# Spreading the last row sums by one product, and sharing the last finishes with ScalarE and GpSimd

## The chip, the cores and the metric

The kernel runs on one core of a Trainium2 chip. Its time is the device time of one execution in microseconds (us), and the number that counts is the median of several executions. A profiled execution of the same program gives the trace: what each engine did and when. The engines are TensorE (PE in the profile, its weight loads PEld), VectorE (DVE), ScalarE (ACT), GpSimd (POOL) and SyncE (SP), which here issues nearly all DMA transfers.

## The reference, cut to what matters

The input x has 2048 rows of 512 numbers. Attention with 32 heads of 16 dimensions each is mixed with a routed feed-forward part by a gate per row:

```python
q, k, v = qkv[0], qkv[1], qkv[2]              # 32 heads, Dh = 16
p = softmax(einsum("bhqd,bhkd->bhqk", q, k) * Dh ** -0.5)
a = einsum("bhqk,bhkd->bhqd", p, v).transpose(0, 2, 1, 3).reshape(B, S, D) @ wo
g = sigmoid((x * gate_w).sum(-1, keepdims=True))
return g * a + (1 - g) * b                    # b: x plus a SwiGLU on the two rows with the largest x @ w_r
```

## The kernel before, in words

**Units and steps.** The 32 heads form 16 pairs. A unit is one pair with one half (1024) of the queries, so there are 32 units, u = 0 to 31 (`UNITS` = 32). A unit has 16 steps, one for each block of 128 keys, 512 steps (`STEPS`) in all. A step makes four score products of 128 keys by 512 queries (`s_piece`, line 596: head j, query chunk c), whose exponentials ScalarE writes to a tile `P` (line 597). Two steps later four products with V (`av_mm`, line 605) add to one PSUM tile `av`. Each of the four takes 32 of its 128 rows; in each such group rows 0 to 15 are the output of one head for one chunk of 512 queries, and row 16 is the row sum of the softmax, because V carries a column of ones. Beside that, up to unit 31, "m" pieces (line 528) and VectorE reductions (line 532) find the row maxima of units to come. A written-out order (`ORDER`) interleaves all of these; `at_step(s, f)` hangs other work behind step s, and a generator `fills` gives one piece of output work per slot. Every engine works through its instructions in the order in which the program gives them.

**The drain.** After the last reduction some 20 steps are left. Each consists of 4 score products, 4 products with V and one `wo_last` (line 453: three products that apply the output weights to 128 rows of the result, into the PSUM tile `fl`, which has one buffer), followed by `finish` on VectorE (line 501: acc = ps * gate + acc). In these steps unit 30, the last but one, is normalized: `l_cols` (line 656) brings its row sums onto the partitions by four small products with `sel_l`, takes the reciprocal of 16 columns (line 658), and copies it out to 512 columns (`rx`, line 660). One step later `l_rows` (line 665) turns `rx` back by four products with the identity, and VectorE multiplies (line 667). `last_rows` (line 672) sends the result by DMA into `last_n[0]`, which `split_last` (line 496) reads later.

**The tail.** `tail()` handles unit 31, for which nothing is left to run beside it. `av_out` copies `av` to an SBUF tile `o` on ScalarE (line 618). Then come the small products (line 693), the reciprocal of 16 columns (line 695), six products of `wo_last`'s kind for row tiles 6 and 7 (`pw`), the copy to 512 columns, half on ScalarE and half on VectorE (lines 701, 702), the turning back into two PSUM tiles (line 705), two multiplications (line 708), and the split of `o` into a rounded part and a rest (`onh` on ScalarE, line 67; `onl` on VectorE, line 68). Then ten row tiles of the output are finished by VectorE (line 501) and stored by SP (`store`, line 504, 128 rows of 2 KB each): first tiles 6 and 7, then the eight tiles 8 to 15, each from three products (line 721) of all 128 rows of `onh` or `onl` with `wz`, the rows of `wo` for the last two heads, with zeros for the rows of the other query chunk.

PSUM tiles: `st` has three buffers, `fl`, `av`, `mxb` one each, `mxa` one of two banks. SBUF tiles of the tag "o" share six buffers.

Of the kernel before, what the change touches and what calls it, by code (L numbers as in the profile page):

```python
# [7 lines left out]
F32 = mybir.dt.float32  # L8
F32R = mybir.dt.float32r
U32 = mybir.dt.uint32  # L10
AF = mybir.ActivationFunctionType
# [5 lines left out]
S, D, H, DH, F = 2048, 512, 32, 16, 1792  # L17
NG = 4
PAIRS = H // 2
UNITS = PAIRS * 2  # L20
KT = S // 128
VW = DH + 1
# [11 lines left out]
def gated_mix(ctx: ExitStack, tc: tile.TileContext, xT, x, wqkv, wo, w_rg, w_gate, w_up, w_down,  # L34
              consts, pos, out):
    nc = tc.nc
    ctx.enter_context(tc.manual_schedule())
    cp = ctx.enter_context(tc.tile_pool(name="cp", bufs=1))
    xp = ctx.enter_context(tc.tile_pool(name="xp", bufs=1))
    ring = ctx.enter_context(tc.tile_pool(name="ring", bufs=1))  # L40
# [6 lines left out]
    def st_tile(shape=(128, 512)):  # L47
        return psum.tile(list(shape), F32, tag="st", name="st", bufs=3)

    def fl_tile(shape=(128, 512)):  # L50
        return psum.tile(list(shape), F32, tag="fl", name="fl", bufs=1)

    def mxa_tile():
        return psum.tile([128, 2, 512], F32, tag="mxa", name="mxa", bufs=1)

    def mxb_tile(shape=(128, 512)):
        return psum.tile(list(shape), F32, tag="mxb", name="mxb", bufs=1)

    def av_tile():
        return psum.tile([128, 512], F32, tag="av", name="av", bufs=1)  # L60

    def o_tile(name, shape, dt=F32):
        return ring.tile(shape, dt, tag="o", name=name, bufs=6)

    def split(hi, lo, src, scale=None, lo_engine=None):
        if scale is None:
            nc.scalar.activation(hi, src, AF.Copy)
            (lo_engine or nc.vector).tensor_sub(lo, src, hi.bitcast(F32))
        else:
            nc.scalar.activation(hi, src, AF.Copy, scale=scale)  # L70
            nc.vector.scalar_tensor_tensor(lo, src, scale, hi.bitcast(F32), op0=OP.mult, op1=OP.subtract)
# [3 lines left out]
        nc.gpsimd.tensor_sub(lo, src, hi.bitcast(F32))  # L75


    cst = cp.tile([128, 135], F32, name="cst")
    ident, sel_j, sel_l, row0 = cst[:, :128], cst[:, 128:130], cst[:, 130:134], cst[:, 134:135]
    V = cp.tile([128, KT, H * VW + 15], F32, name="V")  # L80
    Kx = [cp.tile([128, S], F32R, name=f"Kx{i}") for i in range(2)]
    Qx = [cp.tile([128, S // 2], F32R, name=f"Qx{i}") for i in range(3)]
# [1 line left out]
    gg = cp.tile([128, 16], F32, name="gg")  # L84
# [320 lines left out]
    acc = []  # L405
# [45 lines left out]
    def wo_terms(ps, ah, al, c, sl, first, last):  # L451
        for n, (a, b) in enumerate(((ah, wop[0]), (al, wop[0]), (ah, wop[1]))):
            nc.tensor.matmul(ps, a[:, sl], b[:a.shape[0], c, :], start=first and n == 0, stop=last and n == 2)  # L453
# [30 lines left out]
    lastp = {}  # L484
# [14 lines left out]
    def finish(t, ps):  # L499
        a = acc[t // 4][:, t % 4, :]  # L500
        nc.vector.scalar_tensor_tensor(a, ps, gg[:, t:t + 1], a, op0=OP.mult, op1=OP.add)  # L501

    def store(t):
        nc.sync.dma_start(out[t * 128:t * 128 + 128, :], acc[t // 4][:, t % 4, :])
# [11 lines left out]
    MX, P, AV = {}, {}, {}  # L516
# [82 lines left out]
    def av_mm(s):  # L599
        u, kt = divmod(s, KT)  # L600
        if kt == 0:
            AV[0] = av_tile()
        for ct in range(4):
            h = (u // 2) * 2 + ct // 2
            nc.tensor.matmul(AV[0][32 * ct:32 * ct + 32, :], V[:, kt, h * VW:h * VW + 32], P[s][:, ct, :],  # L605
                             start=kt == 0, stop=kt == KT - 1)
        del P[s]

# [41 lines left out]
        a = last_n[half][:96, q * 512:q * 512 + 512]  # L650
        nc.gpsimd.tensor_mul(a, a, AV["rb", half, q])

    def l_cols(u):
        ps = mxa_tile()[:, 0, :16]
        for c in range(4):
            nc.tensor.matmul(ps[:, 4 * c:4 * c + 4], AV[u][:, c * 128:c * 128 + 128], sel_l, start=True, stop=True)
        r = ring.tile([128, 16], F32, tag="r16", name="r16", bufs=2)
        nc.vector.reciprocal(r, ps)
        AV["rx"] = o_tile("rx", [128, 16, 32])
        nc.vector.tensor_copy(AV["rx"], r[:, :, None].to_broadcast([128, 16, 32]))  # L660

    def l_rows(u):
        ps = mxa_tile()[:, 0]
        for c in range(4):
            nc.tensor.matmul(ps[:, c * 128:c * 128 + 128],
                             AV["rx"][:, 4 * c:4 * c + 4].rearrange("p a b -> p (a b)"), ident, start=True, stop=True)
        nc.vector.tensor_mul(AV[u], AV[u], ps)

    def last_rows():
        for ct in range(4):  # L670
# [3 lines left out]
    wz = []  # L674

    def load_wz(part):
        if part == 0:
            wz.append(ring.tile([128, 2, 2, 512], F32R, tag="xs", name="wz", bufs=2))
            nc.gpsimd.memset(wz[0].bitcast(F32), 0.0)
            return  # L680
        for i in range(2):
            for ct in range(4):
                j, c = divmod(ct, 2)
                nc.sync.dma_start(wz[0][32 * ct:32 * ct + 16, i, c].bitcast(F32),
                                  wop[i][96 + 16 * j:112 + 16 * j, 3].bitcast(F32))

    def tail():
        u = UNITS - 1
        hl = [o_tile(n, [128, 512], F32R) for n in ("onh", "onl")]
        o = AV[u]  # L690
        ps = st_tile((128, 16))
        for c in range(4):
            nc.tensor.matmul(ps[:, 4 * c:4 * c + 4], o[:, c * 128:c * 128 + 128], sel_l, start=True, stop=True)
        r = ring.tile([128, 16], F32, tag="r16", name="rl", bufs=2)
        nc.vector.reciprocal(r, ps)
        rx = o_tile("rxl", [128, 16, 32])
        pw = [st_tile() for _ in range(2)]
        for t in range(2):
            wo_terms(pw[t], lastp[0][0], lastp[0][1], 3, slice((6 + t) * 128, (7 + t) * 128), True, True)
        rb = r[:, :, None].to_broadcast([128, 16, 32])  # L700
        nc.scalar.activation(rx[:, 0:8], rb[:, 0:8], AF.Copy)
        nc.vector.tensor_copy(rx[:, 8:16], rb[:, 8:16])
        pr = [mxb_tile((128, 256)), fl_tile((128, 256))]
        for c in range(4):
            nc.tensor.matmul(pr[c // 2][:, c % 2 * 128:c % 2 * 128 + 128],
                             rx[:, 4 * c:4 * c + 4].rearrange("p a b -> p (a b)"), ident, start=True, stop=True)
        for t in range(2):
            nc.vector.tensor_mul(o[:, 256 * t:256 * t + 256], o[:, 256 * t:256 * t + 256], pr[t])
        for t in range(2):
            sl = slice(256 * t, 256 * t + 256)  # L710
            split(hl[0][:, sl], hl[1][:, sl], o[:, sl])
        for t in range(2):
            finish(6 + t, pw[t])
            store(6 + t)
        two = mxa_tile()
        for c in range(4):
            sl = slice(c * 128, c * 128 + 128)
            for k in range(2):
                ps = (st_tile, lambda: two[:, 0], st_tile, mxb_tile, st_tile, lambda: two[:, 1], st_tile, fl_tile)[2 * c + k]()
                for n, (a, b) in enumerate(((0, 0), (1, 0), (0, 1))):  # L720
                    nc.tensor.matmul(ps, hl[a][:, sl], wz[0][:, b, k, :], start=n == 0, stop=n == 2)
                finish(8 + 4 * k + c, ps)
                store(8 + 4 * k + c)


    fill, now = {}, [0]
# [1 line left out]
    def at_step(s, f, *a):  # L728
        fill.setdefault(s, []).append((f, a))
# [88 lines left out]
    for t in range(6):  # L818
        at_step(STEPS - 6 + t, wo_last, t, 128)
    at_step(400, load_wz, 0)  # L820
    at_step(404, load_wz, 1)

    def p_v(s):
        if not 0 <= s < STEPS:
            return
        av_mm(s)
        if s % KT < KT - 1:
            return
        u, s = s // KT, now[0]
        av_out(u)  # L830
        if u % 8 == 7 and u < 24:
            for i in range(8):
                at_step(s + 6 + i, l_out, u // 8, i)
        elif u == UNITS - 3:
            for i in range(8):
                at_step(s + 3 + i // 2, l_out, 3, i)
            for half in (1, 0):
                for q in range(2):
                    at_step(s + 10 - half, l_last, half, q)
                    at_step(s + 12 - half, n_last, half, q)  # L840
        elif u == UNITS - 2:
            at_step(s + 1, l_cols, u)
            at_step(s + 2, l_rows, u)
            at_step(s + 3, last_rows)

    def start_step(s):
# [30 lines left out]
    while count["m"] < UNITS * EL:  # L877
        for o in ORDER:
            if o == "s":
                s, i = divmod(count["s"], 4)  # L880
# [15 lines left out]
    for s in range(count["s"] // 4, STEPS + 2):  # L896
        if s < STEPS:
            start_step(s)
            for i in range(4):
                s_piece(s, 1 - i % 2, i // 2)  # L900
        p_v(s - 2)
        next(fills, None)
        end_step(s)
    end_step(STEPS + 2)
    assert next(parts, 0) == 0 and not fill and next(fills, 0) == 0, fill
    tail()


# [29 lines left out]
```

## Time and profile before

| | us |
|---|---|
| time, median of 3 runs (lowest to highest) | 1450.44 (1449.56 to 1451.87) |
| the profiled execution's own time | 1449.58 |
| its span, first to last instruction | 1447.8 |
| PE busy | 1430.4 |
| VectorE busy | 1299.6 |
| ScalarE busy | 1164.5 |
| GpSimd busy | 302.6 |

The 1.78 us between the profiled execution's time and its span lie around the first and the last instruction. A timeline row gives the start, the length, engine, line, operation and what it writes and reads; in brackets stands how long the engine had been idle and what ended that. A row of the groups gives a count, the busy time in all, the mean length of one in ns, and the idle time before them. The chain of waits is followed back from the last instruction to what released each step.

### The profile page before, as it was taken

To read this page: it belongs to the slowest core of one execution; us is meant where nothing else is said; L and a number is where in the kernel's file an instruction comes from. 1 tells how busy PE (TensorE), PEld (TensorE's weight loads), DVE (VectorE), ACT (ScalarE), POOL (GpSimd) and SP (SyncE) were. 2 spreads that over 40 slices of the span, in tenths; PEclk is the share of its full clock that TensorE was granted. 3 is DMA by queue.
4 is the path that set the end of the run, shared out by engine and by line. 5 is a ranking of instruction groups with operands and counts; after the bars stand their busy time and mean duration, and the time that the engine had idled before them with its cause. 6 is when DMAs were issued, how large, how long until landed. Compare 5 with 4: busy or idle time off the path is not lost.

```text
span 1447.8 us, 24210 instructions
## 1 busy us (share of the span) xinstructions
PE 1430.4 (99%) x9141; PEld 636.1 (44%) x9141; DVE 1299.6 (90%) x1541; ACT 1164.5 (80%) x2262; POOL 302.6 (21%) x321
## 2 busy tenths in 40 slices
PE   8999999999999999999999999999999999999998
PEld 5654444444444444444444433334444444444434
DVE  5779999999999999999999999999999999999933
ACT  4467888888888888888888888888888888888874
POOL 3652101020010002000010000326322231232120
PEclk9999999999999999999999999999999999999999
DMA  8702121212014121221314242231212120111003
GB/s 264 196 19 63 34 52 45 53 45 51 28 60 114 61 53 31 52 68 50 83 41 107 84 110 67 45 113 51 52 45 53 40 54 20 37 33 38 18 16 117
DMA packets 53476, 92.72 MB, mean 64 GB/s; under 512 B 12972, under 2 KB 24300, under 8 KB 51856
## 3 DMA queue, kind: packets, MB, share of 16 engines
q1 hardware_dynamic: 53264, 91.17, 23.9%
q8 instruction: 72, 1.18, 0.4%
q14 instruction: 44, 0.36, 0.1%
q0 software_dynamic: 96, 0.01, 0.0%
HBM read 63.64 MB, written 28.56 MB: 64 GB/s over the span
## 4 chain that ended last, share of the span: by engine, by line
PE 94%; DMA 2%; DVE 1%; SPq 1%; ACT 1%; issue 0%; POOL 0%; DVEq 0%; ACTq 0%; POOLq 0%
PE av L605 34%; PE st L596 23%; PE mxa L528 12%; PE mxb L528 10%; PE fl L149 6%; PE fl L453 4%; PE st L248 3%; ACT P L597 1%; DMA xs<-xT 1%; SPq L587 1%; PE mxa L555 1%; DVE Mr L532 1%; DMA wvs<-wqkv 0%; PE fl L352 0%; DVE acc L501 0%
## 5 line engine op out<-in xcount | busy, mean ns | idle before, releaser
L597 ACT ACTIVATE P<-st 128x512 f32<-128x512 f32 x2028 | 1065.0, 602 | 217.4 <-PE st L596 127.7
L532 DVE TENSOR_REDUCE Mr<-mxa 128x2 f32<-128x1024 f32 x655 | 794.7, 1213 | 3.9 <-PE mxa L528 3.4
L605 PE MATMUL av<-P,V 128*32 128x512 f32 x4096 | 545.5, 605 | 0.0
L596 PE MATMUL st<-Qx,Kx 50*128 50x512 f32 x2028 | 539.7, 444 | 4.1 <-ACT P L597 3.6
L532 DVE TENSOR_REDUCE Mr<-mxb 128x1 f32<-128x512 f32 x654 | 451.8, 691 | 69.5 <-PE mxb L528 20.1
L596 PEld LDWEIGHTS st<-Qx,Kx 50*128 50x128 f32 x2028 | 280.8, 184 | 238.8 <-ACT P L597 215.2
L528 PE MATMUL mxb<-Kx,Qx 48*128 48x512 f32 x654 | 325.2, 497 | 0.0
L528 PE MATMUL mxa<-Kx,Qx 48*128 48x512 f32 x1310 | 299.2, 420 | 1.0 <-DVE Mr L532 0.8
L528 PEld LDWEIGHTS mxb<-Kx,Qx 48*128 48x128 f32 x654 | 119.5, 183 | 273.7 <-DVE Mr L532 255.2
L528 PEld LDWEIGHTS mxa<-Kx,Qx 48*128 48x128 f32 x1310 | 126.6, 183 | 46.3 <-DVE Mr L532 7.8
L605 PEld LDWEIGHTS av<-P,V 128*32 128x32 f32 x4096 | 80.9, 108 | 146.0 <-issue 140.0
L164 POOL TENSOR_SCALAR ev<-pe 128x512 fp32r<-128x512 f32 x24 | 35.8, 1490 | 375.3 <-ACT pe L163 375.3
L74 POOL TENSOR_SCALAR hl<-m 128x16 fp32r<-128x16 f32 x32 | 8.1, 253 | 384.1 <-DVE m L571 384.0
L420 POOL TENSOR_TENSOR acc<-acc,w 128x512 f32<-128x512 f32 x32 | 41.0, 1281 | 197.4 <-ACT w L419 197.4
L149 PE MATMUL fl<-xh,wh 128*128 128x512 f32 x96 | 42.9, 447 | 0.0
L149 PE MATMUL fl<-xh,wl 128*128 128x512 f32 x96 | 39.6, 413 | 0.0
L453 PE MATMUL fl<-woh,ahl 128*128 128x512 f32 x96 | 35.2, 447 | 0.0
L501 DVE SCALAR_TENSOR_TENSOR acc<-fl,gg,acc 128x512 f32<-128x512 f32 x15 | 11.3, 750 | 26.4 <-PE fl L453 26.4
L560 DVE TENSOR_REDUCE Mr<-mxa 128x2 f32<-128x1024 f32 x21 | 25.7, 1223 | 9.8 <-PE mxa L555 9.8
L149 PE MATMUL fl<-xl,wh 128*128 128x512 f32 x96 | 31.3, 420 | 0.0
L165 POOL TENSOR_TENSOR ev<-pe,ev 128x512 fp32r<-128x512 f32 x24 | 30.8, 1283 | 2.0
L250 ACT ACTIVATE V<-st 128x512 f32<-128x512 f32 x16 | 9.6, 598 | 25.0 <-PE st L248 24.9
(177 smaller groups left out, 780.5 us busy)
## 6 DMA issues: line engine op xcount, KB each, us to landing
Qx<-q_scr SPq DMA_DIRECT2D x62, 128.0 KB
Kx<-k_scr SPq DMA_DIRECT2D x30, 256.0 KB
k_scr<-ev SPq DMA_DIRECT2D x14, 512.0 KB
q_scr<-ev SPq DMA_DIRECT2D x14, 512.0 KB
xs<-xT SPq DMA_DIRECT2D x16, 256.0 KB
xn<-x SPq DMA_DIRECT2D x4, 1024.0 KB
Qx<-hr SPq DMA_DIRECT2D x256, 2.0 KB
acc<-x_scr SPq DMA_DIRECT2D x4, 1024.0 KB
```

The source lines that it names most:

```text
L149: nc.tensor.matmul(ps, a[:, i, c, :], b[nb][:, c, :], start=n == 0, stop=n == 11)
L164: nc.gpsimd.tensor_scalar(ev[:, 0], t, 1.0, None, op0=OP.mult)
L165: nc.gpsimd.tensor_sub(ev[:, 1], t, ev[:, 0].bitcast(F32))
L248: nc.tensor.matmul(ps, a[nb][:, c, sl], b[:, c, :], start=c == 0 and n == 0, stop=c == 3 and n == 2)
L420: nc.gpsimd.tensor_add(a, a, w)
L453: nc.tensor.matmul(ps, a[:, sl], b[:a.shape[0], c, :], start=first and n == 0, stop=last and n == 2)
L528: nc.tensor.matmul(dst, Qx[u % 3][64 * j:64 * j + 48, t * 128:t * 128 + 128], Kx[(u // 2) % 2][64 * j:64 * j + 48, c * 512:c * 512 + 512], ...
L532: nc.vector.tensor_reduce(Mr[:, g0:g0 + (2 if r == 1 else 1)], MX[r - 1], axis=AX.X, op=OP.max, negate=True)
L560: nc.vector.tensor_reduce(*r, axis=AX.X, op=OP.max, negate=True)
L596: nc.tensor.matmul(ps, k, q, start=True, stop=True)
L597: nc.scalar.activation(P[s][:, 2 * j + c, :], ps, AF.Exp)
L605: nc.tensor.matmul(AV[0][32 * ct:32 * ct + 32, :], V[:, kt, h * VW:h * VW + 32], P[s][:, ct, :], start=kt == 0, stop=kt == KT - 1)
```

## The change

- The constant input `consts` grows from 135 to 259 columns. `sel_l` is now 128 columns wide instead of 4: one product with it puts each group's row sum on all 32 rows of the group.
- Unit 30: `l_cols` goes. `l_rows` is one product with `sel_l`, a reciprocal of 128x512 on VectorE and a multiplication on GpSimd instead of VectorE.
- Unit 31: the same with the product, the reciprocal and the multiplication each in two halves of 256 columns; the multiplication stays on VectorE. The products of row tile 6 move ahead of the wait for `o`, into `fl`; those of row tile 7 stand behind the row-sum product.
- The groups of `av` in unit 31 are put in the order chunk, head, so that each chunk has its rows in one half of the partitions. The 24 output products read 48 rows each, from row 0 or from row 64, and alternate between the two halves. `wz` loses the zero half.
- `finish_two` (ScalarE scales PSUM into an SBUF tile, GpSimd adds it to `acc`) takes the place of `finish` for row tiles 6, 7, 12, 13 and 14; tiles 8 to 11 and 15 stay on VectorE. Stores keep their order: 6, 7, 8, 12, 9, 13, 10, 14, 11, 15.

```diff
-    cst = cp.tile([128, 135], F32, name="cst")
-    ident, sel_j, sel_l, row0 = cst[:, :128], cst[:, 128:130], cst[:, 130:134], cst[:, 134:135]
+    cst = cp.tile([128, 259], F32, name="cst")
+    ident, sel_j, row0, sel_l = cst[:, :128], cst[:, 128:130], cst[:, 130:131], cst[:, 131:]
...
-            h = (u // 2) * 2 + ct // 2
-            nc.tensor.matmul(AV[0][32 * ct:32 * ct + 32, :], V[:, kt, h * VW:h * VW + 32], P[s][:, ct, :],
+            j, c = divmod(ct, 2) if u < UNITS - 1 else (ct % 2, ct // 2)
+            h = (u // 2) * 2 + j
+            nc.tensor.matmul(AV[0][32 * ct:32 * ct + 32, :], V[:, kt, h * VW:h * VW + 32], P[s][:, 2 * j + c, :],
                              start=kt == 0, stop=kt == KT - 1)
...
-    def l_cols(u):
...
+    def l_rows(u):
+
+        ps = mxa_tile()[:, 0]
+        nc.tensor.matmul(ps, sel_l, AV[u], start=True, stop=True)
+        r = o_tile("rl", [128, 512])
         nc.vector.reciprocal(r, ps)
...
-        nc.vector.tensor_mul(AV[u], AV[u], ps)
+        nc.gpsimd.tensor_mul(AV[u], AV[u], r)
...
+    def finish_two(t, ps):
+
+        a = acc[t // 4][:, t % 4, :]
+        w = o_tile("wz", [128, D])
+        nc.scalar.activation(w, ps, AF.Copy, scale=gg[:, t:t + 1])
+        nc.gpsimd.tensor_add(a, a, w)
+
     def tail():
+
         u = UNITS - 1
...
+        pw = [fl_tile(), st_tile()]
+        wo_terms(pw[0], lastp[0][0], lastp[0][1], 3, slice(768, 896), True, True)
+        pl = st_tile()
+        for c in range(2):
+            nc.tensor.matmul(pl[:, 256 * c:256 * c + 256], sel_l, o[:, 256 * c:256 * c + 256], start=True, stop=True)
+        wo_terms(pw[1], lastp[0][0], lastp[0][1], 3, slice(896, 1024), True, True)
+        r = o_tile("rl", [128, 512])
+        for c in range(2):
+            sl = slice(256 * c, 256 * c + 256)
+            nc.vector.reciprocal(r[:, sl], pl[:, sl])
+            nc.vector.tensor_mul(o[:, sl], o[:, sl], r[:, sl])
+        for c in range(2):
+            sl = slice(256 * c, 256 * c + 256)
+            split(h[:, sl], l[:, sl], o[:, sl])
         for t in range(2):
...
-            finish(6 + t, pw[t])
+            finish_two(6 + t, pw[t])
             store(6 + t)
...
+        for t in range(4):
+            bank = [[mxb_tile, st_tile, st_tile, av_tile][t](), [st_tile, fl_tile, st_tile, mxb_tile][t]()]
+            for n, (x_, w_) in enumerate(((h, 0), (l, 0), (h, 1))):
+                for c in range(2):
+                    nc.tensor.matmul(bank[c], x_[64 * c:64 * c + 48, t * 128:t * 128 + 128],
+                                     wz[0][64 * c:64 * c + 48, w_, :], start=n == 0, stop=n == 2)
+            for c in range(2):
+                (finish_two if c and t < 3 else finish)(8 + 4 * c + t, bank[c])
+                store(8 + 4 * c + t)
...
-            at_step(s + 1, l_cols, u)
-            at_step(s + 2, l_rows, u)
+            at_step(s + 1, l_rows, u)
             at_step(s + 3, last_rows)
```

More of the change, by code (lines that the diff above doesn't have):

```diff
@@ L651, in n_last @@
         nc.gpsimd.tensor_mul(a, a, AV["rb", half, q])
-    def l_cols(u):
[L654 to L660, printed above, removed]
     def l_rows(u):
         ps = mxa_tile()[:, 0]
-        for c in range(4):
-            nc.tensor.matmul(ps[:, c * 128:c * 128 + 128],
-                             AV["rx"][:, 4 * c:4 * c + 4].rearrange("p a b -> p (a b)"), ident, start=True, stop=True)
-        nc.vector.tensor_mul(AV[u], AV[u], ps)
+        nc.tensor.matmul(ps, sel_l, AV[u], start=True, stop=True)
+        r = o_tile("rl", [128, 512])
+        nc.vector.reciprocal(r, ps)
+        nc.gpsimd.tensor_mul(AV[u], AV[u], r)
     def last_rows():
@@ L677, in load_wz @@
         if part == 0:
-            wz.append(ring.tile([128, 2, 2, 512], F32R, tag="xs", name="wz", bufs=2))
+            wz.append(ring.tile([128, 2, 512], F32R, tag="xs", name="wz", bufs=2))
             nc.gpsimd.memset(wz[0].bitcast(F32), 0.0)
@@ L682, in load_wz @@
             for ct in range(4):
-                j, c = divmod(ct, 2)
-                nc.sync.dma_start(wz[0][32 * ct:32 * ct + 16, i, c].bitcast(F32),
+                j = ct % 2
+                nc.sync.dma_start(wz[0][32 * ct:32 * ct + 16, i].bitcast(F32),
                                   wop[i][96 + 16 * j:112 + 16 * j, 3].bitcast(F32))
+    def finish_two(t, ps):
[3 more added lines that the diff above has]
+        nc.gpsimd.tensor_add(a, a, w)
@@ L687, in tail @@
     def tail():
         u = UNITS - 1
-        hl = [o_tile(n, [128, 512], F32R) for n in ("onh", "onl")]
+        h, l = [o_tile(n, [128, 512], F32R) for n in ("onh", "onl")]
         o = AV[u]
[L691 to L696, printed above, removed]
@@ L697, in tail @@
-        pw = [st_tile() for _ in range(2)]
-        for t in range(2):
[L699 to L712, printed above, removed]
-            finish(6 + t, pw[t])
-            store(6 + t)
[L715 to L723, printed above, removed]
+        pw = [fl_tile(), st_tile()]
@@ L914 @@
     x = np.ascontiguousarray(inputs["A_x"][0])
-    consts = np.zeros((128, 135), np.float32)
+    consts = np.zeros((128, 259), np.float32)
     consts[:, :128] = np.eye(128)
@@ L919 @@
         consts[p % 32 == m, 128 + m] = 1.0
-    for m in range(4):
-        consts[32 * m + DH, 130 + m] = 1.0
-    consts[:, 134] = 128 * p
+    consts[:, 130] = 128 * p
+    for m in range(128):
+        consts[m // 32 * 32 + DH, 131 + m] = 1.0
     arrays = {
```

## The prediction, made before the changed kernel was built or run

> **What bounds the kernel now.** I read the page first, then the timeline of the last 60 us by engine, the windows of the tail, and the groups by form for durations.
>
> ```profile
> PE 1430.4 (99%) x9141; PEld 636.1 (44%) x9141; DVE 1299.6 (90%) x1541; ACT 1164.5 (80%) x2262; POOL 302.6 (21%) x321
> PE 94%; DMA 2%; DVE 1%; SPq 1%; ACT 1%; issue 0%; POOL 0%; DVEq 0%; ACTq 0%; POOLq 0%
> ```
>
> PE bounds the whole, but the change touches the drain and the tail, so each is read by itself. The tail, from its timeline:
>
> ```profile
> 1430.27 1.92 PE L605 MATMUL av<-P,V 128*32 128x512 f32 x16
> 1432.31 0.60 ACT L618 ACTIVATE o<-av 128x512 f32<-128x512 f32 x1 [2.00 <-issue]
> 1432.96 1.06 PE L693 MATMUL st<-cst,o 128*128 128x4 f32 x8 [0.77 <-ACT o L618]
> 1434.06 0.26 DVE L695 RECIPROCAL rl<-st 128x16 f32<-128x16 f32 x1 [2.92 <-PE st L693]
> 1435.35 0.60 PE L705 MATMUL mxb<-cst,rxl 128*128 128x128 f32 x4
> 1435.79 0.61 PE L705 MATMUL fl<-cst,rxl 128*128 128x128 f32 x4
> 1436.05 0.42 DVE L708 TENSOR_TENSOR o<-o,mxb 128x256 f32<-128x256 f32 x1 [1.41 <-PE mxb L705]
> 1436.44 0.42 DVE L708 TENSOR_TENSOR o<-o,fl 128x256 f32<-128x256 f32 x1
> 1436.55 0.76 ACT L67 ACTIVATE onh<-o 128x256 fp32r<-128x256 f32 x2 [1.74 <-DVE o L708]
> 1437.68 2.06 DVE L501 SCALAR_TENSOR_TENSOR acc<-st,gg,acc 128x512 f32<-128x512 f32 x3
> 1443.61 0.74 DVE L501 SCALAR_TENSOR_TENSOR acc<-fl,gg,acc 128x512 f32<-128x512 f32 x1
> ```
>
> From the first L501 on VectorE is never idle: ten finishes, one each 0.66 us ((1443.61 - 1437.68) / 9), to 1444.35. That looks like the bound of the tail. The windows, with the DMA share and GB/s at the right, say otherwise:
>
> ```profile
> core 0: us, PE busy (x) PEld busy (x) DVE busy (x) ACT busy (x) POOL busy (x), PEclk, DMA share, GB/s
> 1438.00:1439.00 1.00, 1.00 (x6) 0.79 (x6) 1.00 (x2) 0.00 (x0) 0.00 (x0) 1.00 0.00 0
> 1439.00:1440.00 1.00, 1.00 (x6) 0.84 (x5) 1.00 (x3) 0.00 (x0) 0.00 (x0) 1.00 0.71 268
> 1445.00:1446.00 1.00, 0.00 (x0) 0.00 (x0) 0.00 (x0) 0.00 (x0) 0.00 (x0) 0.99 0.99 387
> 1446.00:1447.00 1.00, 0.00 (x0) 0.00 (x0) 0.00 (x0) 0.00 (x0) 0.00 (x0) 0.50 0.19 68
> ```
>
> The ten stores of 128 x 512 x 4 = 262 KB keep the DMA engines full from 1439.29 (share 0.71 in that microsecond) to 1446.19 (share 0.19): 6.9 us, 0.68 us a store at 385 GB/s. The first of them can go when the first finish ends, at 1437.68 + 0.74 = 1438.42, and its traffic shows 0.85 us later. So the end is set by when the first stores are released, not by when the last finish ends; making the ten finishes quicker gains nothing unless the first store comes sooner.
>
> **The drain (unit 30).** PE's rows there:
>
> ```profile
> 1392.89 0.73 PE L596 MATMUL st<-Qx,Kx 50*128 50x512 f32 x3
> 1395.36 0.95 PE L656 MATMUL mxa<-cst,o 128*128 128x4 f32 x8
> 1396.24 0.73 PE L596 MATMUL st<-Qx,Kx 50*128 50x512 f32 x3
> 1397.90 0.73 PE L453 MATMUL fl<-woh,lahl 96*128 96x512 f32 x2
> 1398.70 1.05 PE L665 MATMUL mxa<-cst,rx 128*128 128x128 f32 x8
> 1399.68 0.73 PE L596 MATMUL st<-Qx,Kx 50*128 50x512 f32 x3
> 1402.25 0.73 PE L596 MATMUL st<-Qx,Kx 50*128 50x512 f32 x3
> ```
>
> A plain step lasts 2.57 us (1399.68 to 1402.25), the one with L656 3.35, the one with L665 3.44: 0.78 and 0.87 us more, 1.65 in all, and PE is gapless here. The new product is two passes (each fp32 product shows as two matmuls) of 512 columns, 1024 columns in all; L665 is eight of 128, also 1024, so it costs 0.87 again. The drain gains 0.78 us.
>
> What that adds elsewhere: a reciprocal of 512 columns on VectorE and a multiplication on GpSimd. Their prices, from the groups:
>
> ```profile
> L639 DVE RECIPROCAL Lt<-Lt 128x16 f32<-128x16 f32 x24 | 5.8, 242 | 0.0
> L377 DVE RECIPROCAL ffe<-ffe 112x32 f32<-112x32 f32 x1 | 0.3, 342 | 0.0
> L695 DVE RECIPROCAL rl<-st 128x16 f32<-128x16 f32 x1 | 0.3, 257 | 2.9 <-PE st L693 2.9
> L326 DVE RECIPROCAL rsel<-rsel 2x1 f32<-2x1 f32 x1 | 0.2, 151 | 0.0
> L496 DVE CAST lahl<-an 96x512 fp32r<-96x512 f32 x2 | 1.8, 946 | 1.0 <-POOL an L651 1.0
> L496 DVE CAST lahl<-an 128x512 fp32r<-128x512 f32 x2 | 0.8, 416 | 0.0
> L420 POOL TENSOR_TENSOR acc<-acc,w 128x512 f32<-128x512 f32 x32 | 41.0, 1281 | 197.4 <-ACT w L419 197.4
> L419 ACT ACTIVATE w<-fl,gg 128x512 f32<-128x512 f32 x32 | 22.3, 696 | 0.0
> ```
>
> The reciprocal is no streaming operation: 1, 16 and 32 columns take 151, 242 and 342 ns, 6.1 ns a column between the first two and 6.25 between the others. With 6.2 ns, 512 columns take 3.3 us and 256 take 1.73 (+0.015 for a PSUM source, L695 against L639). All four row-sum reciprocals now together take 0.52 us. [...]
>
> Does it hurt the drain? The product ends about 1.05 us after its start near 1395.36, at 1396.4; VectorE is in the reciprocal until 1399.7, then does the delayed finish of the next `wo_last` until 1400.5, which frees `fl`. PE comes to the following `wo_last` at 1396.3 + 2.57 + 1.66 = 1400.5 (1.66 from a step's first row to its L453: 1397.90 - 1396.24). It just meets; I add 0.05 us, bounds 0 and 0.5 (a dearer reciprocal). The multiplication on GpSimd (1.28 us) ends near 1401.1, and `last_rows` sends from there. Its reader has time:
>
> ```profile
> 1400.51 2.48 SPq L672 DMA_DIRECT2D an<-o  x4
> 1410.71 0.42 DVE L496 CAST lahl<-an 128x512 fp32r<-128x512 f32 x1
> ```
>
> The four transfers are now issued by 1403; half a microsecond of delay out of seven is hidden, and nothing else stands in SP's or GpSimd's queue there.
>
> **The tail (unit 31), on the clock of before.** `o` is ready and the row-sum product starts at 1432.96 as now; the products of tile 6 fill PE's wait before it, and those of tile 7 follow, off the path. The product is 4 passes of 256 columns, 1024 columns as in the two L705 rows, which last from 1435.35 to 1436.40: 1.05 us, so the sums are complete at 1434.0, as now. The first half is complete at 0.60, but the two halves share one PSUM bank. No row here shows VectorE reading a bank that PE still writes (the old tail took two tiles for its halves), so the first reciprocal starts between 1433.6 and 1434.06; I take the later, by the old reciprocal's row. [...]
>
> Then in order: reciprocal 1.74 to 1435.80, multiplication 0.42 (L708) to 1436.25, reciprocal to 1438.0, multiplication to 1438.42. ScalarE's queue holds the two `onh` pieces ahead of the new finishes, so its second `onh` piece waits for the second multiplication: 1438.46 to 1438.84. Only now can ScalarE take tile 6, although its product has been ready since 1433: 0.70 us (L419) to 1439.54. GpSimd starts 0.07 later, 1439.6, and adds tiles 6 and 7 by
>
> ```profile
> 1390.90 2.50 POOL L497 TENSOR_TENSOR lahl<-an,lahl 96x512 fp32r<-96x512 f32 x2
> 1393.00 0.75 DVE L501 SCALAR_TENSOR_TENSOR acc<-fl,gg,acc 128x512 f32<-128x512 f32 x1 [1.13 <-PE fl L453]
> ```
>
> (two in 2.50) until 1442.1. Store 6 goes at 1440.9 and store 7 at 1442.14; SP issues in order, so all eight later stores wait behind these. Stores 8 to 15 are then fed two per 1.25 us by GpSimd's adds (the VectorE partner is done long before), 0.62 a store, against the DMA's 0.68. So from store 7 on the transfers run back to back: 1442.14 + 0.85 + 9 x 0.68 = 1449.1, against 1446.19 now: 2.9 us later. (Without the bank wait 2.45; GpSimd's last add ends near 1445.9, its store's traffic is due at 1446.75 and its turn comes at 1447.1.) What it replaces does not show: VectorE's five fewer finishes, the PE time saved by alternating row halves, and the dropped copies and turns, together 2 us from 1434.06 to 1436.05, all lie before or beside this chain, and the new reciprocals alone are 3.5.
>
> **The start.** The constant grows by 62 KB ahead of a 1 MB load on the chain:
>
> ```profile
> cst<-consts SPq DMA_DIRECT2D x1, 67.5 KB
> 13.59 7.24 DMA wvs<-wqkv
> ```
>
> At 385 GB/s that is 0.16 us; I take 0.1, bounds 0 and 0.2. The smaller `wz` memset on GpSimd has slack around it.
>
> **Sum.** -0.78 + 0.05 + 2.9 + 0.1 = +2.3 us. On the profiled execution's 1449.58 that is 1451.9; the median of the runs shown is 0.9 above that execution, so I give 1452.7 against 1450.44, 0.16% more. About 0.2%, 2.9 us, is what a measurement of this kernel can tell from no change.
>
> **The rivals.**
>
> *A, the reciprocal streams like L708* (0.42 us for 256). Then each of the two is 1.3 us shorter, store 7 goes at 1439.5, the tail loses only 0.3, and the whole ends at -0.4: 1450.0, not slower. Three reciprocal rows on one line speak against it. Chance 0.08.
>
> *B, the reciprocal from PSUM costs more per column.* L695 is 15 ns over L639 on 16 columns; if that is 0.94 ns a column and not a fixed step, the tail grows by 0.5 and the drain's meeting at `fl` becomes a stall of about 0.5: +3.3, 1453.7. Nothing but the small size of the step speaks against it. [...] Chance 0.17.
>
> *C, GpSimd's adds and VectorE's finishes exclude each other.* The CAST rows show that it happens: 946 ns beside GpSimd's L651, 416 ns without. If a finish of 0.74 went between adds, two stores would take 1.28 + 0.74 = 2.0 us, five pairs 10.1 from 1439.6, and the last store's traffic would end at 1449.7 + 0.85 + 0.68 = 1451.2: +5.0 in the tail, +4.4 in all, 1454.8. It decides once VectorE holds GpSimd up for over 0.06 x 2 us a pair. Against it: the L501 row at 1393.00 lasted 0.75 with GpSimd busy until 1393.40, whose two adds took the ordinary 2.50. Chance 0.08.
>
> *D, the sum holds*, chance 0.67, with its own range 1451.2 to 1453.8 (start of the first reciprocal 0.45 earlier, the start's 0 to 0.2, a run's scatter of about 1 us by the runs shown).
>
> **How the numbers follow.** The time is D's. The range must reach B and most of C upward and A downward: 1450.3 to 1455.0. Faster by over 0.2% needs A and a further 2.5 us that I see nowhere: 0.04. Slower by over 0.2% (above 1453.3) is B, C and the upper part of D, about a quarter of it: 0.39. The rest, 0.57, lies within 0.2%.
>
> **What would show it.** In the changed profile: the reciprocal rows at 1.74 and 3.3 us (A: 0.4 and 0.7; B: 2.0 and 3.8); GpSimd idle from the end of the drain until about 7 us after the last `av` product, then five adds at 1.25; the DMA share empty until after the first add and at 1.0 from the second on; the drain's two long steps replaced by one of 3.44 us. I am wrong if the DMA is not full after store 7, if ScalarE takes the products of tiles 6 and 7 before the second `onh`, or if the drain shows a wait of PE on `fl` over 0.5 us.

## The result, and the profile after

| | before | after |
|---|---|---|
| median, 22 runs each (lowest to highest), us | 1450.45 (1448.40 to 1454.13) | 1452.18 (1450.55 to 1457.54) |
| ratio after / before, 95% interval | | 1.0015 (1.0009 to 1.0021) |
| the profiled execution's own time, us | 1449.58 | 1453.40 |
| its span, us | 1447.8 | 1451.6 |

The changed kernel is slower by 1.3 to 3.0 us by that interval, which is clear of zero; its middle, 0.15%, is inside the 0.2% that the prediction had set as the border of a real difference. The forecast was 1452.7.

The totals of the profile's page hide this completely: PE's busy time is the same to the tenth of a microsecond.

```profile
span 1451.6 us, 24164 instructions
PE 1430.4 (99%) x9115; PEld 633.1 (44%) x9115; DVE 1302.3 (90%) x1534; ACT 1170.5 (81%) x2266; POOL 309.6 (21%) x327
```

The last microseconds tell it. In the timeline below, the first row is ScalarE's copy of the last `av`, the start of the tail. It stands at 1433.09, where before it stood at 1432.31, so 0.78 us are to be taken off to compare with the predicted clock times.

```profile
1433.09 0.60 ACT L619 ACTIVATE o<-av 128x512 f32<-128x512 f32 x1 [1.99 <-issue]
1433.74 1.13 PE L696 MATMUL st<-o,cst 128*128 128x256 f32 x4
1434.91 1.76 DVE L701 RECIPROCAL rl<-st 128x256 f32<-128x256 f32 x1 [3.00 <-PE st L696]
1436.76 0.42 DVE L702 TENSOR_TENSOR o<-o,rl 128x256 f32<-128x256 f32 x1
1437.10 1.75 DVE L701 RECIPROCAL rl<-st 128x256 f32<-128x256 f32 x1
1438.88 0.43 DVE L702 TENSOR_TENSOR o<-o,rl 128x256 f32<-128x256 f32 x1
1439.34 0.42 ACT L67 ACTIVATE onh<-o 128x256 fp32r<-128x256 f32 x1 [1.66 <-DVE o L702]
1439.67 0.67 ACT L684 ACTIVATE wz<-fl,gg 128x512 f32<-128x512 f32 x1
1440.41 6.20 POOL L685 TENSOR_TENSOR acc<-acc,wz 128x512 f32<-128x512 f32 x5 [24.57 <-ACT wz L684]
1445.44 0.74 DVE L501 SCALAR_TENSOR_TENSOR acc<-mxb,gg,acc 128x512 f32<-128x512 f32 x1
```

Read it from the bottom of the chain: GpSimd's first add of the tail starts at 1440.41, 7.32 us after the copy, because ScalarE takes tile 6 (L684) only after its second `onh` (L67), which waits for the second multiplication, which waits for 1.75 us of reciprocal. The last finish on VectorE ends at 1446.18, 3.8 us before the last transfer does. The windows say what runs in between (the two last columns are the DMA share and GB/s; the one before is PE's granted clock):

```profile
1441.00:1442.00 1.00, 1.00 (x8) 0.80 (x7) 0.71 (x1) 0.68 (x1) 1.00 (x2) 0.50 0.00 0
1442.00:1443.00 1.00, 1.00 (x8) 0.80 (x7) 0.75 (x1) 0.69 (x1) 1.00 (x2) 0.50 0.45 172
1443.00:1444.00 1.00, 1.00 (x8) 0.80 (x6) 0.49 (x1) 0.39 (x1) 1.00 (x1) 0.50 0.44 166
1444.00:1445.00 1.00, 0.74 (x4) 0.03 (x2) 0.49 (x2) 0.30 (x1) 1.00 (x2) 0.71 1.02 383
...
1449.00:1450.00 1.00, 0.00 (x0) 0.00 (x0) 0.00 (x0) 0.00 (x0) 0.00 (x0) 0.50 0.96 375
1450.00:1451.00 1.00, 0.00 (x0) 0.00 (x0) 0.00 (x0) 0.00 (x0) 0.00 (x0) 0.50 0.04 12
```

Store 6 shows at 1442.5, store 7 near 1443.8 after the second add, and from there the transfers are gapless to 1450.0 (a DMA share of 0.96 or more in each microsecond from 1444 on). From the copy's start to the end of the traffic it is 16.87 us, against 13.88 before: the tail has grown by 2.99 us.

The drain, in the timeline. The row-sum product of unit 30 is the two matmuls on L657; where before two steps were long, only the step with L657 is, and the next two are plain, 1397.96 to 1400.51 to 1403.08.

```profile
1392.34 0.50 PE L453 MATMUL fl<-woh,lahl 96*128 96x512 f32 x1 [1.47 <-POOL lahl L497]
1393.01 0.91 PE L596 MATMUL st<-Qx,Kx 50*128 50x512 f32 x3
1397.01 1.02 PE L657 MATMUL mxa<-o,cst 128*128 128x512 f32 x2
1397.96 0.73 PE L596 MATMUL st<-Qx,Kx 50*128 50x512 f32 x3
1398.14 3.36 DVE L659 RECIPROCAL rl<-mxa 128x512 f32<-128x512 f32 x1 [0.18 <-PE mxa L657]
1400.51 0.73 PE L596 MATMUL st<-Qx,Kx 50*128 50x512 f32 x3
1401.57 1.27 POOL L660 TENSOR_TENSOR o<-o,rl 128x512 f32<-128x512 f32 x1 [8.04 <-DVE rl L659]
1403.08 0.73 PE L596 MATMUL st<-Qx,Kx 50*128 50x512 f32 x3
```

That one step is out of line: from 1393.01 it takes 4.95 us, where 3.44 was forecast. The windows give the reason, in the column before the last two:

```profile
1393.00:1394.00 1.00, 1.00 (x9) 0.45 (x12) 0.75 (x1) 0.46 (x1) 0.54 (x1) 0.69 0.00 0
1394.00:1395.00 1.00, 1.00 (x8) 0.05 (x4) 0.00 (x0) 1.00 (x4) 0.00 (x0) 0.50 0.00 0
...
1397.00:1398.00 1.00, 1.00 (x5) 0.23 (x3) 0.75 (x1) 0.00 (x0) 0.00 (x0) 1.00 0.00 0
```

PE's granted clock fell to 0.50 about a microsecond after PE had waited 1.47 us for `lahl`, and stayed low for 3.4 us, to 1396.8. The same products took 1.5 us longer. So the two profiled executions differ by 3.8 us, of which 2.99 is the tail and 0.66 the drain, while the medians differ by 1.7: the pair of profiles overstates the change.

### The profile page after: what moved, and what is told of

It is laid out like the page before. It is cut to its first block, busy times and chain, and to the rows that moved or that the text cites. A ratio compares the mean times of both kernels' runs of the same rounds, so it can differ in the third digit from the quotient of the medians.

```text
span 1451.6 us, 24164 instructions
## 1 busy us (share of the span) xinstructions
PE 1430.4 (99%) x9115; PEld 633.1 (44%) x9115; DVE 1302.3 (90%) x1534; ACT 1170.5 (81%) x2266; POOL 309.6 (21%) x327
## 4 chain that ended last, share of the span: by engine, by line
PE 94%; DMA 2%; DVE 1%; SPq 1%; ACT 1%; POOL 1%; issue 0%; POOLq 0%; ACTq 0%; DVEq 0%
PE av L606 34%; PE st L596 23%; PE mxa L528 12%; PE mxb L528 10%; PE fl L149 6%; PE fl L453 4%; PE st L248 3%; DMA xs<-xT 1%; ACT P L597 1%; SPq L587 1%; PE mxa L555 1%; DMA wvs<-wqkv 1%; DVE Mr L532 1%; PE fl L352 0%; PE st L149 0%
## 5 line engine op out<-in xcount | busy, mean ns | idle before, releaser
L284 ACT ACTIVATE p<-p 128x512 f32<-128x512 f32 x32 | 20.0, 628 | 10.7 <-POOL p L280 10.5
```

## The experiments

For every kernel two lengths were read from its profile. The **drain** runs from the first score product after PE's wait for `lahl` to the start of the copy of the last `av`; the **tail** from there to the end of the stores' traffic. In the expectations T is the account of the prediction (two long reciprocals ahead of the first stores, stores released by GpSimd's adds, then a full DMA); R1 and R2, where they stand, are the rival accounts that the run is put against, with what each would give. The first four kernels were timed beside 35 runs of the kernel before (median 1449.63), the others beside 27 (1449.38). The ratios are those on record with their intervals; they are not the quotient of the two medians, and differ from it by up to 0.0015 (for `e1_no_recip` the medians give 0.9995).

| kernel | median us | ratio to before (95%) | tail us | drain us |
|---|---|---|---|---|
| before | 1450.45 | | 13.88 | 39.42 |
| after | 1452.18 | 1.0015 (1.0009 to 1.0021) | 16.87 | 40.08, low clock |
| `e1_no_recip` | 1448.84 | 0.9980 (0.9965 to 0.9994) | 14.25 | 38.54 |
| `e2_early` | 1450.87 | 1.0001 (0.9989 to 1.0013) | 16.45 | 40.14, low clock |
| `e3_all_dve` | 1450.96 | 1.0003 (0.9990 to 1.0016) | 15.55 | 38.52 |
| `e4_drain` | 1448.78 | 0.9992 (0.9980 to 1.0004) | 13.88 | 38.61 |
| `e5_shared` | 1449.55 | 1.0001 (0.9990 to 1.0013) | 14.44 | 39.41 |
| `e6_two_banks` | 1451.34, one run | | 16.48 | 38.54 |
| `e7_best` | 1446.67 | 0.9984 (0.9974 to 0.9994) | 12.68 | 40.19, low clock |
| `e8_best_late` | 1445.81 | 0.9974 (0.9965 to 0.9984) | 12.68 | not readable (no wait) |

**The reciprocals' cost by itself.** From the changed kernel; unit 31's division is left out, a copy of the same shape stands in its place.

```diff
-            nc.vector.reciprocal(r[:, sl], pl[:, sl])
+            nc.vector.tensor_copy(r[:, sl], pl[:, sl])
```

> The changed kernel with the two reciprocals of 256 columns in the tail replaced by copies (the reciprocal of unit 31's row sums is left out). Theory T: the end is set by when the adds of row tiles 6 and 7 release their stores; those stand behind both reciprocals, so two times 1.75 - 0.42 = 2.7 us earlier, and the whole ends 2.7 us below the changed kernel, 0.9 us below the kernel before (ratio to before 0.9994). Rival R1, the five GpSimd adds at 1.25 us are the price by themselves: they too start 2.7 us earlier, so no difference from T here. Rival R2, PE at half its clock in the tail sets the end: PE's wait for its first piece shrinks, the clock stays up, and the products take 0.7 instead of 1.3 us a tile: over 3 us less.

The tail fell by 2.62 us, to 14.25. A copy of 256 columns is 0.42 us where the reciprocal is 1.75, so 2 x 1.33 = 2.66 was to go, and went. The reciprocals are the bulk of the tail's growth; what is left over against the kernel before is 0.37. The ratio came out lower than T gave, with an interval that reaches T's 0.9994; no low clock shows in this kernel's drain. The clock stayed at 1.00 through the products of this tail too, as R2 says, and R2's "over 3 us" is not far from 2.62, so this run alone does not put R2 aside.

**Tiles 6 and 7 ahead of the reciprocals.** From the changed kernel:

```diff
+        for t in range(2):
+            finish_two(6 + t, pw[t])
+            store(6 + t)
         r = o_tile("rl", [128, 512])
         for c in range(2):
...
-        for t in range(2):
-            finish_two(6 + t, pw[t])
-            store(6 + t)
```

> The changed kernel with the two shared finishes of row tiles 6 and 7 and their stores moved ahead of the reciprocals, so that ScalarE takes them while it waits; every instruction stays. T: store 6 leaves near 7 us after the last product with V less, at about 1436, store 7 by 1438; then the end hangs on stores 8 to 15: store 8 leaves when VectorE's first finish ends (about 1441.7 on the changed kernel's clock), the next add on GpSimd 1.3 later, and eight stores at 0.68 end near 1448.6 instead of 1450.0: 1.4 us below the changed kernel, ratio to before 1.0005. R1: the last GpSimd add ends at best 1 us earlier, so at most 1 us. R2: no gain, since PE's products are not touched.

A miss: the tail lost 0.42 us where T gave 1.4. The timeline says why (VectorE's two multiplications, GpSimd's add of tile 7, and its three adds of tiles 12 to 14):

```profile
1435.43 1.26 POOL L685 TENSOR_TENSOR acc<-acc,wz 128x512 f32<-128x512 f32 x1 [0.42 <-ACT wz L684]
1435.77 1.20 DVE L705 TENSOR_TENSOR o<-o,rl 128x256 f32<-128x256 f32 x1
1438.67 0.42 DVE L705 TENSOR_TENSOR o<-o,rl 128x256 f32<-128x256 f32 x1
1441.60 3.78 POOL L685 TENSOR_TENSOR acc<-acc,wz 128x512 f32<-128x512 f32 x3 [4.91 <-ACT wz L684]
```

The first multiplication lasts 1.20 us instead of 0.42, with GpSimd's add beside it from its start to 1436.69, 0.28 us before its end. The 0.78 us more are put down to that add, and the second reciprocal stands behind them. And the deciding store is another one now. With 6 and 7 long gone, the fourth store in SP's order, tile 12, waits for GpSimd's add at 1441.60, and seven stores are still to go from there. That add ends 10.76 us after the copy, where T's figures put it at about 9.9 (1443.0 on the changed kernel's clock); the 0.78 is most of the difference. Moving the early stores only handed the end to the next shared one. PE's low clock, 0.50 in the microseconds from 1438, is on this path: from the first product with `onl` to VectorE's first finish it was 1.26 us, against 0.77 at full clock in `e6_two_banks`. R1's "at most 1 us" fits the 0.42 as well as T does; what tells the two apart stands with the next run.

**All finishes on VectorE.** From the changed kernel:

```diff
-            finish_two(6 + t, pw[t])
+            finish(6 + t, pw[t])
...
-                (finish_two if c and t < 3 else finish)(8 + 4 * c + t, bank[c])
+                finish(8 + 4 * c + t, bank[c])
```

> The changed kernel with all ten finishes on VectorE again (the share of ScalarE and GpSimd undone, all else kept). T: VectorE finishes tile 6 right after its second piece of onl, at 1441.0, and tile 7 at 1441.6; ten stores at 0.68 from 1441.0 + 0.85 end at 1448.6, 1.4 us below the changed kernel, though VectorE's last finish (about 1447) ends later than now (1446.2): ratio to before 1.0005. R1 expects a gain of the same sign; R2 none. If instead VectorE was the bound of the tail, as its gapless finishes suggest, this is slower than the changed kernel by about 1 us.

The tail fell by 1.32, as T said. VectorE's timeline, first and last finish; the copy of the last `av` starts at 1432.56 here:

```profile
1439.61 0.75 DVE L501 SCALAR_TENSOR_TENSOR acc<-fl,gg,acc 128x512 f32<-128x512 f32 x1
1445.63 0.74 DVE L501 SCALAR_TENSOR_TENSOR acc<-mxb,gg,acc 128x512 f32<-128x512 f32 x1
```

The last finish ends 13.81 us after the copy, later than in the changed kernel (1446.18 - 1433.09 = 13.09), and yet the tail is shorter: the first store is released at 7.80 instead of 8.6. So sharing the finishes costs 1.3 us on this kernel, and the engine that it relieves was not the bound. R2 expected no gain, and the clock is at 0.50 from 1439 on in this tail too: PE's clock does not set the end. R1 expects the same sign as T here. Against it stand the windows of the changed kernel: adds that set the pace would leave holes in the transfers, and from 1444 to 1450 there are none.

**The drain's part alone.** From the kernel before; its tail keeps the narrow selector, so the constant has both (263 columns).

```diff
+        nc.tensor.matmul(ps, sel_w, AV[u], start=True, stop=True)
+        r = o_tile("rl", [128, 512])
+        nc.vector.reciprocal(r, ps)
+        nc.gpsimd.tensor_mul(AV[u], AV[u], r)
...
-            at_step(s + 1, l_cols, u)
-            at_step(s + 2, l_rows, u)
+            at_step(s + 1, l_rows, u)
```

> The kernel before with the drain's part of the change alone (unit 30: one row-sum product with the wide constant, a reciprocal of 512 columns, the multiplication on GpSimd); the tail is the old one. T: PE's two long steps of 3.35 and 3.44 us become one of 3.44 and one of 2.57, 0.8 us less, with a wait of PE on fl of 0.1 us at most: ratio to before 0.9995. Rival: the reciprocal of 3.36 us holds VectorE and so fl, PE waits 0.5 us or more, and the gain is 0.3 or less.

The drain is 0.81 us shorter and the tail is as before, 13.88. PE's and VectorE's rows:

```profile
1394.16 1.02 PE L656 MATMUL mxa<-o,cst 128*128 128x512 f32 x2
1395.11 0.73 PE L596 MATMUL st<-Qx,Kx 50*128 50x512 f32 x3
1395.29 3.36 DVE L658 RECIPROCAL rl<-mxa 128x512 f32<-128x512 f32 x1 [0.18 <-PE mxa L656]
1397.66 0.73 PE L596 MATMUL st<-Qx,Kx 50*128 50x512 f32 x3
```

The 3.36 us on VectorE delay nobody: the next step starts 2.55 us after the last. By the ratio alone it could be no change; the profile carries the verdict.

**Sharing alone.** The kernel before, with `finish_two` of the change for three of the ten tiles:

```diff
-                finish(8 + 4 * k + c, ps)
+                (finish_two if k and c < 3 else finish)(8 + 4 * k + c, ps)
```

> The kernel before, with three of its ten last finishes (row tiles 12, 13, 14) given to ScalarE and GpSimd and nothing else changed: the sharing alone, without delaying the first store. T: the DMA engines are the bound from the first store on, so the tail keeps its 13.9 us (from the copy of the last av to the end of the stores), within 0.2, though VectorE's last finish ends about 1.5 to 2 us sooner: ratio to before 1.000. Rival, VectorE's finishes are the bound of the old tail: 2 us less, ratio 0.9986.

VectorE's last finish ends 11.50 us after the copy instead of 12.04, only 0.54 sooner where T had 1.5 to 2, because two of its last three finishes wait 0.6 us each for their products; and the tail grows by 0.56. The rival in which VectorE bounds the tail falls, since its last finish came sooner and the end later. T's 13.9 was 0.5 too low, outside the 0.2 it allowed, since it had left out what the windows show, a hole in the transfers while tile 12 waits for GpSimd's add (GpSimd is the column with 0.92):

```profile
1439.00:1440.00 1.00, 1.00 (x6) 0.80 (x5) 0.58 (x1) 0.48 (x1) 1.00 (x1) 1.00 1.01 379
1440.00:1441.00 1.00, 1.00 (x6) 0.84 (x5) 0.75 (x1) 0.27 (x2) 0.92 (x2) 1.00 0.54 205
```

**The bank.** From the changed kernel, the two row-sum products in banks of their own:

```diff
-        pl = st_tile()
+        pl = [st_tile((128, 256)), mxa_tile()[:, 0, :256]]
```

> The changed kernel with the two halves of the last row-sum product in two PSUM banks instead of one. T: the first reciprocal then starts when the first half is done, 0.4 to 0.45 us earlier after the copy of the last av (1.4 instead of 1.82 us), and the tail shrinks from 16.9 to 16.4 to 16.5 us. Rival: the wait was for something else (the whole product's pipeline), and the start stays at 1.82.

In the timeline the first reciprocal starts while PE is still at the second half:

```profile
1431.42 0.60 ACT L619 ACTIVATE o<-av 128x512 f32<-128x512 f32 x1 [2.00 <-issue]
1432.61 0.59 PE L696 MATMUL mxa<-o,cst 128*128 128x256 f32 x2
1432.81 1.76 DVE L701 RECIPROCAL rl<-st 128x256 f32<-128x256 f32 x1 [2.57 <-PE st L696]
```

It starts 1.39 us after the copy instead of 1.82, and the tail is 0.39 shorter. The wait for both halves in one bank, on which the prediction had chosen the later of two values, is real and worth 0.4 us. The halves were also parts of one tile and are two tiles now. Parts of an SBUF tile are waited for singly here (in after the first `onh` starts at 1437.26, before the second multiplication touches the other half of `o` at 1438.88), which speaks for the bank; whether the chip or the order built into the program holds VectorE back, no run shows.

**What the theory asks for.** Keep the drain's part and the old tail, and release stores 6 and 7 early, on VectorE: tile 6's products and finish go ahead of the reciprocal of 16 columns, tile 7's products behind the row-sum products and its finish behind the copies to `rx`. From `e4_drain`:

```diff
+        pw = [fl_tile(), st_tile()]
+        wo_terms(pw[0], lastp[0][0], lastp[0][1], 3, slice(768, 896), True, True)
         ps = st_tile((128, 16))
...
+        finish(6, pw[0])
+        store(6)
+        wo_terms(pw[1], lastp[0][0], lastp[0][1], 3, slice(896, 1024), True, True)
...
+        finish(7, pw[1])
+        store(7)
...
-        for t in range(2):
-            finish(6 + t, pw[t])
-            store(6 + t)
```

> The tail of the kernel before with the products of row tile 6 ahead of the wait, and the finishes of tiles 6 and 7 on VectorE in the gaps it has before the two multiplications, their stores right behind; with the drain's part of the change. T: stores 6 and 7 leave at about 1.7 and 3.3 us after the copy of the last av starts, the chain to the first output product is 0.4 us shorter, and the eight other stores run back to back from about 1438.1 on the old clock: end of the stores near 1444.4, tail 12.1 instead of 13.9; with the drain's 0.8 the whole is 2.6 us below the kernel before, ratio 0.9982. Rival: VectorE has no room there, the finishes push the multiplications back by 1.3 us, and only the drain's 0.8 is left.

VectorE's finishes of tiles 6, 7 and 8 and the last one:

```profile
1433.07 0.75 DVE L501 SCALAR_TENSOR_TENSOR acc<-fl,gg,acc 128x512 f32<-128x512 f32 x1 [1.99 <-PE fl L453]
1434.80 0.75 DVE L501 SCALAR_TENSOR_TENSOR acc<-st,gg,acc 128x512 f32<-128x512 f32 x1 [0.22 <-PE st L453]
1437.81 0.75 DVE L501 SCALAR_TENSOR_TENSOR acc<-st,gg,acc 128x512 f32<-128x512 f32 x1 [0.48 <-PE st L714]
1442.59 0.75 DVE L501 SCALAR_TENSOR_TENSOR acc<-fl,gg,acc 128x512 f32<-128x512 f32 x1
```

The tail is 12.68, 1.2 below the kernel before; T had said 12.1, too low because the finish of tile 8 waits for its product until 1437.81. The rival falls: the first multiplication starts 3.36 us after the copy, against 3.74 in the kernel before. The kernel beats the one before and the changed one. In its drain the granted clock fell once more, after a wait for `lahl` of 1.01 us.

**Without the wait for `lahl`.** From `e7_best`, the last eight `wo_last` start one step later:

```diff
-        yield from wait(STEPS - 15)
+        yield from wait(STEPS - 14)
```

> The same as the one before, and in addition the eight output products of the first drain steps start one step later, so that PE does not stand before them waiting for GpSimd's lahl (0.7 to 1.5 us in the profiles so far; where it was 1.4 or more, the granted clock fell to 0.5 for some 3 us and cost 1.5 us more). T: the wait goes, the clock stays at 1.0 in every profile, at least 0.8 us less than the kernel without this: ratio to before 0.9975 or less, and a narrower scatter from run to run. Rival: the step that is moved finds the same wait one step later, since the transfers it hangs on are late by more than a step; no gain.

The first `wo_last` with `lahl` in PE's timeline has no wait behind it:

```profile
1391.63 0.74 PE L453 MATMUL fl<-woh,lahl 96*128 96x512 f32 x2
```

The median is 1445.81, the ratio 0.9974 (0.9965 to 0.9984), and the runs lie within 1.9 us of each other. It is the fastest kernel of this study, 0.41% or 5.9 us below the changed one by the difference of the two ratios. The intervals of this kernel and `e7_best` overlap, so what this line is worth by itself is not settled; that it removes the wait is.

**One formula for all tails.** The tail is the time at which the deciding store's finish ends, counted from the copy, plus 0.85 us until its traffic shows, plus 0.68 us for it and each store behind it. The deciding store is the one for which this sum is largest.

| kernel | deciding store: its finish ends | stores from there | computed | measured |
|---|---|---|---|---|
| before | 6: 6.11 | 10 | 13.76 | 13.88 |
| after | 7: 9.82 | 9 | 16.79 | 16.87 |
| `e1_no_recip` | 7: 7.16 | 9 | 14.13 | 14.25 |
| `e2_early` | 12: 10.76 | 7 | 16.37 | 16.45 |
| `e3_all_dve` | 6: 7.80 | 10 | 15.45 | 15.55 |
| `e5_shared` | 14: 11.49 | 3 | 14.38 | 14.44 |
| `e6_two_banks` | 7: 9.40 | 9 | 16.37 | 16.48 |
| `e7_best` | 8: 6.31 | 8 | 12.60 | 12.68 |

For instance after: GpSimd starts at 1440.41, its second add ends 2.50 later, 9.82 us after 1433.09. All eight come out 0.06 to 0.12 us below the measured length, with one duration of a store and one delay taken from the kernel before. Some decisions are close: in `e5_shared` tiles 12 and 13 give 14.3 as well, and in `e7_best` every store from 8 on gives 12.60 to 12.62, since VectorE's finishes are 0.68 apart there, a store's own time. In that kernel the finishes and the DMA engines limit the tail alike.

## Why the prediction was right, point by point

- **The drain, -0.78 + 0.05.** Measured -0.81 in `e4_drain`, with no stall on `fl`, and -0.88 to -0.90 in `e1_no_recip`, `e3_all_dve` and `e6_two_banks`, which have the changed drain and no fall of the clock in it. The step held to 0.1 to 0.2 us.
- **The reciprocal, 6.2 ns a column.** 1.75 and 1.76 us for 256 columns (1.74 said), 3.36 for 512 (3.3 said). That is rival A refuted by its own row, and rival B too: from PSUM a column costs 6.3 ns between these two lengths, where B needs 7.1.
- **The bank wait.** The later start was taken; after shows it (1.82 us after the copy, 1.75 in the prediction) and `e6_two_banks` shows what removes it.
- **ScalarE's order and GpSimd's start.** Forecast 1439.6 on the old clock, 1440.4 with the shift of 0.78; the row says 1440.41. Five adds in 6.20, as said.
- **The DMA full after store 7, tail +2.9.** Measured +2.99; forecast end 1449.1 + 0.78 = 1449.9, traffic ends at 1450.0.
- **Rival C.** VectorE's finishes beside GpSimd's adds last 0.75 us as ever, also those at 1440.95 and 1442.23:

```profile
1440.95 0.75 DVE L501 SCALAR_TENSOR_TENSOR acc<-mxb,gg,acc 128x512 f32<-128x512 f32 x1 [0.73 <-PE st L713]
1442.23 0.75 DVE L501 SCALAR_TENSOR_TENSOR acc<-st,gg,acc 128x512 f32<-128x512 f32 x1 [0.53 <-PE fl L713]
```

  It falls for these finishes, which read one operand from PSUM. (The 946 ns that spoke for this rival was the mean of two casts, 1481 ns beside GpSimd's L651 and 412 behind it.) Two instructions of VectorE did last longer beside one of GpSimd: the multiplication with both operands in SBUF in `e2_early` (1.20 us instead of 0.42), and the cast just named, which reads one operand, in SBUF. Which forms are slowed beyond these is not shown.
- **The start, +0.1.** Not seen. The load of `wvs` starts at 13.59 us before and at 13.30 after and lasts 7.24 and 7.83 us, and the changed kernel was the earlier by 0.6 at 1376 us. This term stays open.
- **The sum.** Tail and drain without the low clock (+2.99 and -0.81 to -0.90) make +2.1 to +2.2 of the +2.3 forecast; the medians gave +1.7, and 1.3 to 3.0 by the interval. The forecast of 1452.7 stands 0.5 above the measured median. That it came so close is in part luck, because single executions move by more than that with the clock, which the sum did not have.
- **Slips without weight.** The 0.52 us are the two row-sum reciprocals L658 and L695, not four. The chances of B, C and a quarter of D add to 0.42, not 0.39.
- **What the prediction did not have** is the clock's fall in the drain, 1.5 us in some executions. The wait for `lahl` ahead of it is not set by the edited code of the drain, which comes later, and it was 0.80 us in `e1_no_recip`, whose program is the same up to the tail, against 1.47 in after. One profile of a kernel does not show how often the clock falls, but the mean granted clock of each execution is on record. Of the 22 of the changed kernel 15 had 0.994 or less and took 1450.95 to 1457.54 us (median 1453.04), and 7 had more and took 1450.55 to 1451.63 (median 1450.79). Of the 62 of the kernel before that were timed beside the experiments, 47 had 0.997 or more and took 1447.08 to 1450.93, and 15 had less and took 1450.49 to 1456.90. So falls of the clock go with the long times of both. The changed kernel's spell at 0.50 in the tail, 6.8 us, is in its mean as well (about 0.002), and the mean does not say where the clock fell, so it stays open whether the change makes the fall in the drain more frequent. Which length of wait brings it is open as well: there was none after 0.74, 0.78, 0.80, 0.82 and 0.95 us, one after 1.01, 1.44 and 1.47, and none after 1.39 in `e5_shared`.

## What to carry to other kernels

In the eight tails of the table, which end in a row of stores that fill the DMA, the end is the release of the deciding store plus the stores behind it, to 0.12 us: ask which store decides before making anything quicker. Relieving the engine that finishes last gained nothing here (`e5_shared`: its last finish 0.54 us sooner, the tail 0.56 us longer), and spreading the finishes over ScalarE and GpSimd cost 1.3 us where it delayed an early store (`e3_all_dve` against after). Spreading first and inverting later multiplied the work of a reciprocal that took 6.2 ns a column: 16 columns of reciprocal took 0.26 us and the copy to 512 columns 0.29 on VectorE beside 0.42 on ScalarE, against 2 x 1.75 for 512 columns of reciprocal. Order a tail so that whatever needs no result of the last stage is stored before that stage begins: with stores 6 and 7 early on VectorE the tail was 12.68 us instead of 13.88 (`e7_best`).

## What the runs showed of the hardware

- In the drain the granted clock of PE fell to 0.50 in three profiles, 1.0 to 2.0 us after the end of a wait of 1.01, 1.44 or 1.47 us. It stayed there for 3.4 us each time (after 1393.4 to 1396.8, `e2_early` 1393.3 to 1396.7, `e7_best` 1393.0 to 1396.4), which cost about 1.5 us. In the changed tail the clock was at 0.50 from 1437.8 to 1444.6, after 2.1 us without products; a pair of output tiles then took PE 1.28 us instead of 0.69 in `e1_no_recip`, off the path there and on it in `e2_early`.
- Two products of 48 rows in different halves of the partitions ran side by side: at full clock (`e1_no_recip`) the six products of a pair of tiles took three rounds 0.23 us apart, the time of three products of 128 rows in the kernel before.
- A VectorE multiplication with both operands in SBUF took 1.20 us instead of 0.42 beside one GpSimd add (`e2_early`).
- A finish by ScalarE and GpSimd takes 0.67 + 1.26 us one after the other, 2.0 with the hand-over (`e2_early`, tile 7: 1434.66 to 1436.69), against 0.75 on VectorE. No run here had VectorE alone as the bound, so what such a trade gains there is not shown.
